# Token lists of a mixture-of-experts kernel built by one-hot matrix products instead of scatters, with the first expert's late columns in fp32 and a reordered start of the last layer

## The chip, the cores and the metric

One core of one Trainium2 chip. The metric is the device time of one execution in microseconds, as the median of several runs. Engines are named as in the profile: PE is TensorE (matmuls), DVE is VectorE, ACT is ScalarE, POOL is GpSimd, SP is SyncE, which here only issues DMAs.

## What is computed

Retention attention over 2 batches x 8 heads x 768 positions x 64, whose output, as 1536 tokens of 512 numbers, goes through a noisy top-2 mixture of eight experts (512 to 1024 to 512), and then through a dense layer with SoLU and layer norm. All in fp32.

```python
def _attn_ref(q, k, v):
    ...
    for t in range(S):
        state = gamma[None, :, None, None] * state + np.einsum('bhd,bhe->bhde', k[:, :, t], v[:, :, t])
        y[:, :, t] = scale * np.einsum('bhd,bhde->bhe', q[:, :, t], state)

def _moe_ref(x, w_gate, w_noise, noise, w1, w2):
    noisy_logits = x @ w_gate + np.log1p(np.exp(x @ w_noise)) * noise
    top2 = np.argpartition(-noisy_logits, 2, axis=1)[:, :2]
    ...
    for e in range(E):
        for k in range(2):
            mask = top2[:, k] == e
            h = np.maximum(x[mask] @ w1[e], 0.0)
            out[mask] += top2_w[mask, k, None] * (h @ w2[e])

def _moe2_ref(x, w_in, w_out, g_ln):
    h = x @ w_in
    e = np.exp(h - np.max(h, axis=-1, keepdims=True))
    solu = h * (e / (np.sum(e, axis=-1, keepdims=True) + 1e-09))
    ...
    ln = (solu - mu) / np.sqrt(var + 1e-06) * g_ln
    return ln @ w_out
```

## The kernel before

The 1536 tokens are twelve tiles of 128. The order of instructions on every engine is the order in which the program writes them; nothing is rescheduled. Each engine takes its own in order.

**Attention and routing.** A loop over the twelve tiles (i = 0 to 11) makes the scores, adds the running state, and lets `rows_logits` multiply by the gate (L461), store the rows of x to `xd` in DRAM and keep the logits. `choose` (L472 to L503) picks the top two of four groups of tiles: 0 to 3, 4 to 7, 8 and 9, 10 and 11. `rank` counts, with products against triangular and full matrices of ones, how many earlier tokens chose the same expert. `slots` (L589 to L603, seven VectorE operations) turns rank and expert into an address in a list `token_of` in DRAM, and `scatter` (L652) lets POOL write 128 token numbers of four bytes there, twice a tile, 24 times in all, each behind a one-element memset. `load_xg` (L959) later reads a list of an expert back (L968), scales it (L974), and gathers the tokens' rows of x by it (L983).

**The first expert** doesn't wait for its list. Its tokens of tiles 0 to 7 (192 columns, "early") and of tiles 8 to 11 (256, "late") are found by one-hot products: `first_rows` compares ranks with column numbers (L527, 16-bit one-hot tiles), `list_rows` (L530) multiplies them with token numbers (L539), POOL gathers (L548), TensorE transposes (L561). The early columns are multiplied in plain fp32 with the raw weights, four matmuls for each of eight steps f of the hidden layer (L671), while routing goes on. The late ones, like all other experts, use pairs of f32r numbers, hi and lo: twelve matmuls a step (hi x hi, hi x lo, lo x hi), with weights split by ScalarE (`wh`, L202) and VectorE (`wl`, L203). Each step's result leaves its PSUM bank as `hh` on ScalarE (L675) and `hl` on VectorE (L676); two banks `b` take turns. Then comes the second layer (`second`, L1038), between and behind whose parts the next expert's rows are transposed (L997).

**Seven more experts**, sorted by how many tokens they have, run the same way with a list each. The last one's second layer leaves rows (L1127, three blocks of 128 tokens, banks c3, c2, c0), stored by `y_rows` (L1110, L1112).

**Last layer.** POOL gathers each token's two expert rows (L766), `mix` weighs and adds them (ScalarE L776, VectorE L777), `x2_t` transposes (L786) and splits them (L789, L790), `h_in` multiplies by w_in (L805, 24 matmuls a tile in two halves), `solu_max`/`solu` (L810 to L824), `z_t` transposes (L858), `z_turn` (L869) does the same through DRAM for later tiles, `out_mm` multiplies by w_out (L915). The last four row blocks of w_out are scaled and split late, by `last_weights` (L901, L902), from two loads of 512 KB.

Weights come in units of 512 KB on SP's queue (`load_unit`, L184); `feed(split_to, load_to)` splits and loads up to given units.

## Time and profile before

| | us |
|---|---|
| median of 3 runs (lowest to highest) | 541.91 (539.79 to 543.49) |
| the profiled execution | 540.02 |
| its span, first to last instruction | 538.3 |
| TensorE busy in it | 504.6 (94%) |
| VectorE, ScalarE, POOL busy | 372.5, 218.7, 190.8 |
| mean granted TensorE clock | 0.974 |

All trace times below are from that one execution, counted from its first instruction; 1.7 us lie outside its span. [...]

### The profile page before, as it was taken

The numbers are of one execution on the slowest core, as the hardware profiler recorded it, in microseconds if no ns is written. First come the engines' busy times: TensorE is split into PE (matmuls) and PEld (weight loads), VectorE is DVE, ScalarE is ACT, GpSimd is POOL, SyncE is SP. The second block draws the span as 40 slices with busy tenths as digits, with TensorE's granted clock in tenths as the row PEclk, the third lists the DMA queues.
The fourth block names the chain that finished last, engine by engine and source line by source line (L and its number), as shares of the span: only waits on it lengthen the run. The fifth ranks groups of instructions, "written<-read, shape, count | busy, mean of one in ns | idle before, by whom it ended". The sixth has DMA issues, their size and how long they took to land.

```text
span 538.3 us, 8946 instructions
## 1 busy us (share of the span) xinstructions
PE 504.6 (94%) x3216; PEld 459.6 (85%) x3216; DVE 372.5 (69%) x742; ACT 218.7 (41%) x426; POOL 190.8 (35%) x287
## 2 busy tenths in 40 slices
PE   8998769399999999999999999999799999999995
PEld 7777659399999999999999999998577888888885
DVE  4468737277688968878988889886148865667640
ACT  4656215053432433424343434435235553343441
POOL 3015435657671732704827100000423523311120
PEclk9999959799999999999999999999989999999999
DMA  8996603468486674866876757666632665553331
GB/s 246 324 329 193 226 20 122 153 196 291 141 274 198 237 214 131 294 161 209 262 260 216 202 190 221 185 173 176 226 86 66 195 202 146 159 173 99 97 118 44
DMA packets 60130, 100.36 MB, mean 186 GB/s; under 512 B 10896, under 2 KB 28400, under 8 KB 60080
## 3 DMA queue, kind: packets, MB, share of 16 engines
q1 hardware_dynamic: 52720, 85.94, 50.7%
q0 software_dynamic: 6016, 13.44, 8.8%
q8 instruction: 27, 0.44, 0.3%
q10 hardware_dynamic: 1344, 0.34, 0.3%
q14 instruction: 23, 0.19, 0.1%
HBM read 76.99 MB, written 22.70 MB: 185 GB/s over the span
## 4 chain that ended last, share of the span: by engine, by line
PE 82%; DMA 6%; DVE 4%; another core or an unknown queue 3%; issue 2%; ACT 1%; POOL 0%; SPq 0%; POOLq 0%; ACTq 0%; DVEq 0%
PE c L1038 24%; PE b L671 14%; PE b L915 12%; PE a L671 12%; PE d L805 11%; PE c L461 2%; PE b L407 1%; DMA y<-yg,slot_y 1%; PE c L449 1%; PE c L1127 1%; DMA qt<-in_qT_dram 1%; PE a L786 1%; DMA xr<-xd,rows 1%; PE c L671 1%
## 5 line engine op out<-in xcount | busy, mean ns | idle before, releaser
L983 POOL DMA_INDIRECT xq<-xd,rows x78 | 91.2, 1169 | 65.9 <-issue 65.3
L203 DVE TENSOR_TENSOR wl<-wr,wh 128x1024 fp32r<-128x1024 f32 x68 | 81.5, 1218 | 3.7 <-ACT wh L202 3.2
L1038 PE MATMUL c<-hh,wh 128*128 128x448 f32 (+5 forms) x224 | 78.8, 352 | 0.0
L1038 PE MATMUL c<-hh,wl 128*128 128x448 f32 (+5 forms) x224 | 78.8, 352 | 0.0
L1038 PE MATMUL c<-hl,wh 128*128 128x448 f32 (+5 forms) x224 | 78.7, 352 | 0.0
L202 ACT ACTIVATE wh<-wr 128x1024 fp32r<-128x1024 f32 x68 | 69.9, 1050 | 6.5 <-DMA wr<-in_moe_w_dram 5.2
L766 POOL DMA_INDIRECT y<-yg,slot_y x24 | 23.6, 985 | 93.4 <-DMA yg<-y 87.8
L671 PE MATMUL b<-xh,wh 128*128 128x256 f32 (+7 forms) x144 | 48.4, 342 | 8.7 <-DVE hl L676 8.6
L671 PE MATMUL b<-xh,wl 128*128 128x256 f32 (+7 forms) x144 | 47.7, 337 | 0.0
L805 PE MATMUL d<-wh,x2h 128*128 128x512 f32 x96 | 40.0, 417 | 3.3 <-ACT x2h L789 3.3
L1038 PEld LDWEIGHTS c<-hh,wl 128*128 128x128 f32 x224 | 42.1, 188 | 1.1
L1038 PEld LDWEIGHTS c<-hh,wh 128*128 128x128 f32 x224 | 42.1, 188 | 1.1
L1038 PEld LDWEIGHTS c<-hl,wh 128*128 128x128 f32 x224 | 42.1, 188 | 1.1
L675 ACT ACTIVATE hh<-b 128x256 fp32r<-128x256 f32 (+8 forms) x40 | 18.5, 466 | 58.8 <-PE b L671 32.4
L805 PE MATMUL d<-wh,x2l 128*128 128x512 f32 x96 | 39.0, 406 | 0.0
L671 PE MATMUL a<-xh,wh 128*128 128x448 f32 (+6 forms) x112 | 38.9, 348 | 0.0
L805 PE MATMUL d<-wl,x2h 128*128 128x512 f32 x96 | 38.8, 405 | 0.0
L671 PE MATMUL a<-xh,wl 128*128 128x448 f32 (+6 forms) x112 | 38.8, 347 | 0.0
L1003 ACT ACTIVATE xh<-xt 128x428 fp32r<-128x428 f32 (+5 forms) x24 | 13.0, 540 | 58.7 <-DVE xt L1001 55.4
L676 DVE SCALAR_TENSOR_TENSOR hl<-b,hh 128x256 fp32r<-128x256 f32 (+8 forms) x40 | 20.9, 524 | 22.4 <-ACT hh L675 16.6
L671 PEld LDWEIGHTS b<-xh,wh 128*128 128x128 f32 x144 | 28.0, 194 | 9.5 <-DVE hl L676 9.1
L832 POOL TENSOR_SCALAR st<-st 128x1 f32<-128x1 f32 x12 | 2.5, 205 | 84.9 <-ACT ee L829 84.8
(226 smaller groups left out, 1110.6 us busy)
## 6 DMA issues: line engine op xcount, KB each, us to landing
wr<-in_moe_w_dram SPq DMA_DIRECT2D x64, 512.0 KB
zd<-zs SPq DMA_DIRECT2D x40, 128.0 KB
zc<-zd SPq DMA_DIRECT2D x10, 512.0 KB
raw<-in_moe_w_in_dram SPq DMA_DIRECT2D x8, 512.0 KB
raw<-in_moe_w_out_dram SPq DMA_DIRECT2D x8, 512.0 KB
yg<-yr SPq DMA_DIRECT2D x16, 208.0 KB
qt<-in_qT_dram SPq DMA_DIRECT2D x12, 256.0 KB
vt<-in_v_dram SPq DMA_DIRECT2D x12, 256.0 KB
```

Source lines behind the costliest of these rows:

```text
L202: nc.scalar.activation(hi, t, AF.Copy)
L203: nc.vector.tensor_sub(lo, t, hi)
L461: nc.tensor.matmul(rows[:, at:at + 128 + 2 * E], XT[i][:, s, k, :], unit[:, s, k, :], start=(k == 0), stop=(k == 1), skip_group_check=True)
L671: nc.tensor.matmul(p, w[:, 0, f * 128:(f + 1) * 128], x[:, d, c], start=(n == 0), stop=(n == len(terms) - 1))
L675: nc.scalar.activation(hh[:, f, c], p, AF.Relu)
L676: nc.vector.scalar_tensor_tensor(hl[:, f, c], p, 0.0, hh[:, f, c], op0=OP.max, op1=OP.subtract)
L766: nc.gpsimd.indirect_dma_start(out=t, out_offset=None, in_=yg[:upto], in_offset=bass.IndirectOffsetOnAxis(ap=slot_y[:, i, s:s + 1], axis=0))
L805: nc.tensor.matmul(PH[i][:, s, :], x[:, c], w[:, 0, f], start=(n == 0), stop=(n == 3 * KD - 1))
L915: nc.tensor.matmul(p, z[:, f * 128:(f + 1) * 128], w_rows(f, n)[:, c], start=(m == 0), stop=(m == len(terms) - 1))
L983: nc.gpsimd.indirect_dma_start(out=x[:, b] if e > 1 else xr_t[e][b], out_offset=None, in_=src[:], in_offset=bass.IndirectOffsetOnAxis(ap=r ...
L1003: nc.scalar.activation(hi, t, AF.Copy)
L1038: nc.tensor.matmul(py[d][:, :CAPS[e]], c, h[:, f, :CAPS[e]], start=(f == 0 and n == 0), stop=(f == KF - 1 and n == 2))
```

## The change

**Lists.** The scatters, `slots`, the DRAM list and its reads are gone. One PSUM bank ("books") holds ranks, counts and the first expert's row numbers, and in it 24 products of 128x128 one-hot tiles (L632) build all lists: for each tile and choice, `columns` makes two tiles of 16-bit numbers on VectorE, one with the token number where the list and set agree (L625), one with 1 where the place in the set agrees (L626). `places` prepares their scalars once for all tiles, `pick_rows` takes the second expert's rows (four operations) and then the others' (six) out of the bank. `turns` counts with one product instead of twelve. The columns are written between the first expert's late steps.

**First expert.** The late 256 columns are multiplied in fp32 with the raw weights too, so its four first-layer units are not split, and their raw tiles live in the buffers of `wl`. Its transposed rows are copied, not split. The second layer's four units are loaded during tiles 10 and 11. The second expert's transposes move from the fourth part of the second layer to behind parts 2, 3, 3 and 4.

**Last layer.** The third block uses bank c3 instead of c0. `mix(1)` stands behind the block loop, and so does the load of the last two weight units. The first half of `h_in(0)` takes the hi terms first. All `last_weights` come after `z_turn(1)`.

```diff
-        t = wraw.tile([128, a, n], F32, tag="wr", name="wr")
+        t = wsp.tile([128, a, n], F32, tag="wl", name="wr") if u < 4 else wraw.tile([128, a, n], F32, tag="wr", name="wr")
...
-    feed_at = [0, 0]
+    feed_at = [4, 0]
...
-        hi, lo = xgT[0]
         at = BLKS[2 * part][0]
-        nc.scalar.activation(hi[:, d:d + 2, at:at + 2 * n], p, AF.Copy)
-        nc.vector.tensor_sub(lo[:, d:d + 2, at:at + 2 * n], p, hi[:, d:d + 2, at:at + 2 * n])
-
-    xe = rt.tile([128, KD, EARLY], F32, name="xe", bufs=1)
-    ROWP, RK, x0, xgT = {}, {}, {}, {}
-
-    def rank(g, tag):
+        if d:
+            nc.scalar.activation(xe[:, d:d + 2, at:at + 2 * n], p, AF.Copy)
+        else:
+            nc.vector.tensor_copy(xe[:, d:d + 2, at:at + 2 * n], p)
+
+    xe = px.tile([128, KD, CAP], F32, tag="xh", name="xe")
+    x0, xgT = {}, {}
+    books = []
+    RK = None
...
+    def open_books():
+
+        nonlocal RK
+        p = bank("a1")
+        books.extend((p[:, 0:4], p[:, 4:100], p[:, 128:224], p[:, 256:384]))
+        RK = books[2].rearrange("p (i e) -> p i e", e=E)
...
-    def slots(g):
-        (t, pk), p = RT.pop(g), RK[g]
-        i0, m = GROUPS[g]
-        ii = slice(i0, i0 + m)
-        rk, at, spare = ranks[:, ii, :], t[:, 6, :m, :2], t[:, 7, :m, :2]
+
+    sq = const.tile([128, E, E], F32, name="sq")
+
+    def turns():
+
         V = nc.vector
-        V.tensor_mul(pk[:, :m], pk[:, :m], p[:, :, None, :].to_broadcast([128, m, 2, E]))
-        V.reduce_sum(rk, pk[:, :m], axis=AX.X)
-
-        V.tensor_scalar(sets[:, ii, :], rk, 1 / 32, -31 / 64, op0=OP.mult, op1=OP.add)
-        V.scalar_tensor_tensor(at, top_i[:, ii, :], ROOM / 16, rk, op0=OP.mult, op1=OP.add)
-        V.scalar_tensor_tensor(at, sets[:, ii, :], (1 - ROOM) / 16, at, op0=OP.mult, op1=OP.add)
-
-        V.scalar_tensor_tensor(spare, rk, float(ROOM), behind[:, ii, :], op0=OP.is_ge, op1=OP.mult)
-        V.scalar_tensor_tensor(slot[:, ii, :], at, 16.0, spare, op0=OP.mult, op1=OP.max)
...
+        nc.tensor.matmul(p, ones, chosen.rearrange("p i e -> p (i e)"), start=False, stop=True, skip_group_check=True)
...
+    def places():
+
+        V = nc.vector
+        full = [128, NT, 2, E]
+        pk = ep.tile([128, CAP], F32, tag="xt", name="pk", bufs=2)
+        pk = pk[:, :NT * 2 * E].rearrange("p (i s e) -> p i s e", s=2, e=E)
+        v = ep.tile([128, NT, 2], F32, name="v")
+        rj = ep.tile([128, NT, 2], F32, name="rj")
+        V.tensor_copy(top_i, ix[:, :, :2])
+        V.tensor_tensor(pk, e8[:, None, None, :].to_broadcast(full), top_i[:, :, :, None].to_broadcast(full),
+                        op=OP.is_equal)
+        V.tensor_mul(pk, pk, RK[:, :, None, :].to_broadcast(full))
+        V.reduce_sum(ranks, pk, axis=AX.X)
+        V.tensor_scalar(sets, ranks, 1 / 32, -31 / 64, op0=OP.mult, op1=OP.add)
+        V.scalar_tensor_tensor(rj, sets, -32.0, ranks, op0=OP.mult, op1=OP.add)
+        V.tensor_scalar(v, sets, 15.0, None, op0=OP.min)
+        V.scalar_tensor_tensor(v, top_i, 16.0, v, op0=OP.mult, op1=OP.add)
+        lw = ep.tile([128, 24, 128], F16, tag="yr", name="lw")
+        LS["v"], LS["rj"], LS["w"] = v, rj, lw
+
+    def columns(ks):
+        for k in ks:
+            i, s = divmod(k, 2)
+            o, w = LS["w"][:, k % 12], LS["w"][:, 12 + k % 12]
+            nc.vector.tensor_scalar(w, lane_h, LS["v"][:, i, s:s + 1], number_f[:, i:i + 1], op0=OP.is_equal, op1=OP.mult)
+            nc.vector.tensor_scalar(o, lane_4.rearrange("p a j -> p (a j)"), LS["rj"][:, i, s:s + 1], None, op0=OP.is_equal)
+            LS[k] = o, w
+
+    def lists(ks):
+        for k in ks:
+            i, s = divmod(k, 2)
+            nc.tensor.matmul(books[3], *LS.pop(k), start=False, stop=(k == 2 * NT - 1), skip_group_check=True)
+
+    def pick_rows(one):
+
+        V = nc.vector
+        got = books[3].rearrange("p (e b) -> p b e", b=16)
+        if one:
+            m, n = [128, 16, E], [128, 4, 4]
+            t = ep.tile([128, CAP], F32, tag="xt", name="t1", bufs=2)
+            t = t[:, :16 * E].rearrange("p (b e) -> p b e", e=E)
+            u = ep.tile([128, 16], F32, name="u1")
+            V.tensor_mul(t, got, sq[:, 1:2, :].to_broadcast(m))
+            V.reduce_sum(u, t, axis=AX.X)
+            u = u.rearrange("p (b c) -> p b c", c=4)
+            V.tensor_mul(u, u, own[:, None, :].to_broadcast(n))
+            V.reduce_max(rows1, u, axis=AX.X)
+            return
+        m = [128, 3, 16, E]
+        for n in (0, 3):
+            t = ep.tile([128, CAP], F32, tag="xt", name="t2", bufs=2)
+            t = t[:, :48 * E].rearrange("p (n b e) -> p n b e", b=16, e=E)
+            u = ep.tile([128, 3, 16], F32, tag="u2", name="u2")
+            V.tensor_mul(t, got[:, None].to_broadcast(m), sq[:, 2 + n:5 + n, None, :].to_broadcast(m))
+            V.reduce_sum(u, t, axis=AX.X)
+            V.tensor_scalar(rows2[:, n:n + 3], u, 4.0, part, op0=OP.mult, op1=OP.add)
...
-    def scatter(i):
-        for s in range(2):
-            nc.gpsimd.memset(spacer, 0.0)
-            st = nc.gpsimd.indirect_dma_start(
-                out=token_of[:], out_offset=bass.IndirectOffsetOnAxis(ap=slot[:, i, s:s + 1], axis=0),
-                in_=token[:, i:i + 1], in_offset=None)
-            for o in scat:
-                tc.declare_no_dep(st.ins, o.ins, reason="slots are distinct")
-            scat.append(st)
...
+        if e:
+            xh, xl = xgT[e]
+            terms = [(unit_t[8 * e + d][n], x, d) for x, ns in ((xh, (0, 1)), (xl, (0,))) for d in range(KD) for n in ns]
+        else:
+            terms = [(raw_t[d], xe, d) for d in range(KD)]
...
-    SCATTER = {6: (0,), 7: (1,), 8: (2,), 9: (3,), 10: (4,), 11: (5,)}
...
-        for n in SCATTER.get(i, ()):
-            scatter(n)
-        feed(0, max(0, min(2 * (i - 7), 4)))
+        feed(0, max(0, min(2 * (i - 7), 8)))
...
+        terms = [(x, d, n) for d in range(KD) for x, n in ((hi, 0), (hi, 1), (lo, 0))]
+        if s == 0 and i == 0:
+
+            terms.sort(key=lambda t: t[0] is lo)
...
     for f in range(KF):
         evacuate = hidden(0, f, slice(0, EARLY), ("c0", "c1", "b", "b")[f % 4])
         if f == 1:
-            list_rows(1, range(NT - 2), "a0")
+            list_rows(1, range(NT - 2))
         if f == 2:
-            rank(3, "c3")
+            rank(3)
             first_rows(3)
         if f == 3:
             list_rows(1, range(NT - 2, NT))
-            slots(2)
-            for n in range(7, 10):
-                scatter(n)
         evacuate()
-        if f > 2:
-            feed(min(f - 2, 4), 0)
-    feed(4, 8)
+        if f == 4:
+            route(2)
+            route(3)
+        if f == 5:
+            turns()
+        if f == 6:
+            places()
     for p in range(2):
         first_xt(1, 2 * p)
-    route(3)
-    slots(3)
-    scatter(10)
-    scatter(11)
-    turns()
...
+        if e == 1:
+            xr_t[e] = []
+            for b in range(4):
+                n = min(128, CAPS[1] - 128 * b)
+                t = px.tile([128, DM], F32, tag="xr", name="xr", bufs=4)
+                nc.gpsimd.indirect_dma_start(out=t[:n], out_offset=None, in_=xd[:],
+                                             in_offset=bass.IndirectOffsetOnAxis(ap=rows1[:n, b:b + 1], axis=0))
+                xr_t[e].append((t, n))
+            return
...
+        up = 8 * e + AHEAD[j] if e else 5 + j if j < 4 else 1 + 2 * j if j < 7 else 14
         if j > (3 if e else 1):
             convert()
-        feed(up, up + 3)
+        feed(up, up + (3 if e else 4))
...
+                if not e:
+                    columns(range(6 * f, min(6 * f + 6, 2 * NT)))
+                    lists(range(max(0, 6 * f - 6), min(6 * f, 2 * NT)))
+                    if f == 5:
+                        pick_rows(True)
+                        for _ in load_xg(1):
+                            pass
+                    if f == 6:
+                        pick_rows(False)
...
-            second(e, j, py, (0, 1) if j == 3 and not e else ())
-            for d in (((0, 1), (2,), (3,), ()) if e else ((), (), (), (2, 3)))[j]:
+            second(e, j, py)
+            for d in (((0, 1), (2,), (3,), ()) if e else ((), (0,), (1, 2), (3,)))[j]:
                 xg_t(e + 1, d)
...
-        py = bank(("c3", "c2", "c0")[b])
+        py = bank(("c3", "c2", "c3")[b])
...
-            feed(n_units - 2, n_units)
             mix(0)
-            mix(1)
+    mix(1)
+    feed(n_units - 2, n_units)
...
     solu(0)
-    last_weights((0, 1))
     x2_t(2)
     h_in(1, 0)
     h_in(1, 1)
@@ -1153,7 +1160,7 @@
     z_t(0)
     solu(1)
     z_turn(1)
-    last_weights((2, 3))
+    last_weights(range(4))
```

Of the order of instructions, POOL between the last scatters and the gathers of the third expert (before): `xr` and `xq` are gathered rows of x, `token_of` is the list in DRAM.

```order
L654 MEMSET spacer 1x1
L655 DMA token_of<-token,slot 7168x1
L968 DMA rows<-token_of,at_r 128x4
L983 DMA xr<-xd,rows 128x512 x4
L968 DMA rows<-token_of,at_r 128x16
L974 TENSOR_SCALAR rows<-rows,part 128x16
L983 DMA xq<-xd,rows 128x128 x14
```

The same place after the change, from the last operation of attention on:

```order
L390 TENSOR_TENSOR vs<-vt,dec 128x256 x11
L535 DMA xr<-xd,rows_166 96x512 x2
L535 DMA xr<-xd,rows_166 128x512 x2
L980 DMA xr<-xd,rows_248 128x512 x3
L980 DMA xr<-xd,rows_248 64x512
L989 DMA xq<-xd,rows_249 128x128 x78
```

The spacers, scatters, list reads and scalings are gone; what remains are the gathers.

VectorE, before, from the end of `turns` over the first expert's late steps (`hl` is a step's low half, `wl` a weight's):

```order
L619 TENSOR_TENSOR keys<-best,over 128x8
L620 TENSOR_REDUCE short<-keys 128x1
L621 TENSOR_REDUCE spill<-short 128x1
L676 SCALAR_TENSOR_TENSOR hl<-b,hh 128x256 x4
L203 TENSOR_TENSOR wl<-wr,wh 128x1024
L676 SCALAR_TENSOR_TENSOR hl<-b,hh 128x256 x2
L203 TENSOR_TENSOR wl<-wr,wh 128x1024
L676 SCALAR_TENSOR_TENSOR hl<-b,hh 128x256 x2
```

And after, at the end of the columns (`lw` are the one-hot tiles, `a_787` the bank of lists, `rows_248` the second expert's rows):

```order
L625 TENSOR_SCALAR lw<-lane_h,v,number_f 128x128
L626 TENSOR_SCALAR lw<-lane_173,rj 128x128
L200 TENSOR_TENSOR wl<-wr,wh 128x1024
L703 SCALAR_TENSOR_TENSOR hl<-b,hh 128x256 x2
L643 TENSOR_TENSOR t_1555<-a_787,sq 128x128
L644 TENSOR_REDUCE u_1556<-t_1555 128x16
L646 TENSOR_TENSOR u_1556<-u_1556,own 128x16
L647 TENSOR_REDUCE rows_248<-u_1556 128x4
L200 TENSOR_TENSOR wl<-wr,wh 128x1024
L703 SCALAR_TENSOR_TENSOR hl<-b,hh 128x256
```

The late steps' `hl` now stand among 48 `lw` operations and the taking out of the rows, and fewer `wl` stand there.

ScalarE, before, at the end of the last expert (`y<-c` empties a block's bank, `t` is the mix of tile 0, then tile 1, `x2h` the transposed rows of tile 0, then tile 1):

```order
L1110 ACTIVATE y<-c_4320 128x4x4x32
L776 ACTIVATE t<-y_4308,top_w 128x512
L776 ACTIVATE t<-y_4312,top_w 128x512
L789 ACTIVATE x2h<-a_4380 128x512
L1110 ACTIVATE y<-c_4358 128x4x4x32
L789 ACTIVATE x2h<-a 128x512
```

And after:

```order
L1118 ACTIVATE y<-c_4210 128x4x4x32
L796 ACTIVATE t<-y_4198,top_w 128x512
L809 ACTIVATE x2h<-a_4263 128x512
L1118 ACTIVATE y<-c_4241 128x4x4x32
L796 ACTIVATE t<-y_4202,top_w 128x512
L809 ACTIVATE x2h<-a 128x512
```

The second `t` moved from ahead of the first `x2h` to behind it and behind the third block's `y`.

## Rows read from the trace of the kernel before

**Rows 1.** The page, part 4: the chain, share of the span by engine.
```profile
PE 82%; DMA 6%; DVE 4%; another core or an unknown queue 3%; issue 2%; ACT 1%; POOL 0%; SPq 0%; POOLq 0%; ACTq 0%; DVEq 0%
```

**Rows 2.** Busy time of each engine in five stretches (start:end us).
```profile
core 0: us, PE busy (x) PEld busy (x) DVE busy (x) ACT busy (x) POOL busy (x), PEclk, DMA share, GB/s
40.00:50.00 10.00, 8.57 (x145) 7.30 (x144) 9.36 (x38) 5.77 (x24) 5.68 (x10) 1.00 0.75 240
70.00:80.00 10.00, 6.73 (x24) 6.04 (x25) 4.13 (x24) 2.04 (x8) 2.13 (x5) 0.50 0.08 27
90.00:100.00 10.00, 4.89 (x46) 4.26 (x44) 6.55 (x29) 1.72 (x4) 8.26 (x16) 1.00 0.89 324
120.00:370.00 250.00, 250.00 (x1344) 244.69 (x1343) 206.00 (x339) 97.64 (x143) 98.51 (x87) 1.00 0.69 214
390.00:400.00 10.00, 10.00 (x39) 7.96 (x39) 2.74 (x4) 2.01 (x3) 3.96 (x4) 0.78 0.43 125
```

**Rows 3.** Chain of waits, 55 to 140 us (start, length, what).
```profile
67.94 6.23 another core or an unknown queue
...
92.75 10.45 another core or an unknown queue
...
114.95 17.02 PE c L1038 x84
```

**Rows 4.** Timeline of POOL, 58 to 105 us (start, length, instruction).
```profile
62.68 1.03 POOL L655 DMA_INDIRECT token_of<-token,slot  x1 [0.18 <-issue]
...
71.61 0.96 POOL L655 DMA_INDIRECT token_of<-token,slot  x1 [0.22 <-issue]
...
88.78 1.13 POOL L655 DMA_INDIRECT token_of<-token,slot  x1 [0.23 <-issue]
...
100.55 0.96 POOL L655 DMA_INDIRECT token_of<-token,slot  x1 [0.22 <-issue]
```

**Rows 5.** Timeline of DVE, 55 to 90 us.
```profile
57.14 1.07 DVE L527 TENSOR_SCALAR oh<-col_h,s 128x448 f16<-128x448 f16 x4
58.13 0.18 DVE L481 TENSOR_TENSOR lg<-lgs 128x32 f32<-128x32 f32 x1
...
63.73 0.21 DVE L595 TENSOR_TENSOR pk<-pk,a 128x64 f32<-128x64 f32 x1
...
64.87 0.17 DVE L485 SCALAR_TENSOR_TENSOR rt<-rt 128x16 f32<-128x16 f32 x1
...
83.73 0.48 DVE L527 TENSOR_SCALAR oh<-col_h,s 128x256 f16<-128x256 f16 x2
84.12 0.35 DVE L676 SCALAR_TENSOR_TENSOR hl<-b,hh 128x192 fp32r<-128x192 f32 x1
```

**Rows 6.** Timeline of PE, 76 to 93 us.
```profile
76.83 4.50 PE L671 MATMUL c<-xe,wr 128*128 128x192 f32 x16
...
87.53 2.76 PE L671 MATMUL b<-xe,wr 128*128 128x192 f32 x16
...
92.31 0.39 PE L671 MATMUL b<-xh,wh 128*128 128x256 f32 x1
```

**Rows 7.** The page, part 5: the group of weight splits on DVE.
```profile
L203 DVE TENSOR_TENSOR wl<-wr,wh 128x1024 fp32r<-128x1024 f32 x68 | 81.5, 1218 | 3.7 <-ACT wh L202 3.2
```

**Rows 8.** Timeline of PE, 385 to 405 us.
```profile
388.46 0.80 PE L805 MATMUL d<-wh,x2h 128*128 128x512 f32 x1 [3.29 <-ACT x2h L789]
...
394.14 0.72 PE L786 MATMUL a<-ident,t 128*128 128x128 f32 x4
...
397.49 0.60 PE L786 MATMUL a<-ident,t 128*128 128x128 f32 x4
...
404.95 0.66 PE L858 MATMUL a<-ident,z 128*128 128x128 f32 x4 [0.84 <-DVE x2l L790]
```

**Rows 9.** Chain of waits, 370 to 425 us.
```profile
379.76 7.36 DMA y<-yg,slot_y
```

**Rows 10.** Timeline of DVE at 403 us.
```profile
402.89 1.41 DVE L902 SCALAR_TENSOR_TENSOR xl<-wr,gcol,xh 128x512 fp32r<-128x512 f32 x2
```

More of the change, by code (lines that the diff above doesn't have):

```diff
@@ L493, in choose @@
         V.tensor_add(nl, nl, lg[:, :, :E])
-        ix = rt.tile([128, 4, 8], U32, tag="ix", name="ix", bufs=3)
         for n in range(m):
@@ L538, in list_rows @@
                 at, n = BLKS[2 * part + b]
-                nc.tensor.matmul(p[:n, b:b + 1], OH[i][:, at:at + n], number[:, i:i + 1], start=(i == 0 and b == 0),
+                nc.tensor.matmul(p[:n, b:b + 1], OH[i][:, at:at + n], number[:, i:i + 1], start=False,
                                  stop=last, skip_group_check=True)
@@ L557, in first_xt @@
         n = BLKS[2 * part][1]
-        p = bank("ab"[1 - part], (128, 2, 2 * n)) if n <= 128 else None
+        p = bank(f"c{2 + d // 2}" if part else "b", (128, 2, 2 * n))
         for s in range(2):
@@ L623, in weights @@
+    rows1 = const.tile([128, 4], U32, name="rows1")
+    rows2 = const.tile([128, E - 2, 16], U32, name="rows2")
     def weights():
@@ L927, in retnet_moe_solu @@
     hidden_of(0)
-    route(3)
-    route(2)
-    route(3)
-    route(3)
-    scatter(6)
-    raw0 = [raw_t[d] for d in range(KD)]
+    for n in range(3):
+        route(3)
     for f in range(KF):
@@ L994, in xg_t @@
             t = bank("a")
[L995 to L997 removed]
+            for b, (x, n) in enumerate(xr_t[e]):
+                nc.tensor.transpose(t[:, 128 * b:128 * b + n], x[:n, d * 128:(d + 1) * 128], ident[:n, :n])
         else:
@@ L1027, in y_t, with second @@
             PY.pop(e)
-    def second(e, j, py, between=()):
+    def second(e, j, py):
         hh, hl = H_t[e]
```

169 lines of the change are left out of this document (58 added, 111 removed).

## Prediction

> **What bounds the kernel now.** I read the page's chain by engine first, then the windows of engine time, then the chain of waits piece by piece where TensorE is idle, and last the timelines of single engines. The chain says that TensorE sets the end for 82% of the span, and that 3% stands against "another core or an unknown queue" [rows 1]. There is only one core, so those 3% are waits whose releaser the profile could not name, and they deserve a look. The windows show where TensorE is not busy: from 120 to 370 us it is busy 250.00 of 250.00 us at granted clock 1.00, but only 6.73 of 10 in 70 to 80, at 0.50, and 4.89 of 10 in 90 to 100; 390 to 400 is full but at 0.78 [rows 2]. The middle, seven experts, therefore gives nothing unless TensorE gets less to do there, and the change leaves its matmuls alone. What can be won lies in three places: the end of attention, the first expert's late columns, and the step from the last expert to the last layer.
>
> The chain of waits gives the two unnamed pieces: 6.23 us from 67.94 and 10.45 us from 92.75, together 16.7 us [rows 3]. In both, VectorE and ScalarE wait for TensorE results whose matmuls had been issued before. Both lie inside a burst of scatters on POOL: the first burst starts at 62.68 with eight scatters and its last one at 71.61, the second at 88.78 with ten and its last at 100.55 [rows 4]. The first unnamed piece ends at 74.17, the second at 103.20, each some 2 us after its last scatter began. That is a coincidence in time seen twice, not a mechanism; no row says why a list write on POOL should hold TensorE's results. It is not the DMA engines' time: in 70 to 80 their share is 0.08 [rows 2]. It is not POOL's indirect DMAs as such: POOL is busy 98.51 us in the experts, with gathers, and TensorE has no gap there [rows 2].
>
> [...]
>
> **The change part by part.** The sums are made against the profiled execution, 540.02 us.
>
> *End of attention.* All 24 scatters go. The 6.23 us piece should go with them. The seven VectorE operations that made scatter addresses go too: at tile 11 they take VectorE from 63.73 to 64.87, 1.14 us [rows 5], in front of the routing chain that ends just where the unnamed piece begins, so they are on the path. The same seven stand at tile 6, where VectorE is busy 9.36 of 10 us [rows 2]; I count 0.8 of those 1.1. In their place an index search of four tiles moves from tile 10 to tile 11, on the same crowded engine, which I count as even. Together 8.2 us. From below: if only the stall goes and the search costs what the slots did, 6.2; from above, both sets of slots in full, 8.5. The two weight units of the second layer that are now loaded during tiles 10 and 11 are on SP's queue among the x stores; that queue carries only what is needed later, so I count nothing; if a store that a gather needs came 1 us later it would cost that 1 us.
>
> *First expert, early columns.* Same matmuls. Sixteen of them take 4.50 us at 76.83, right after the idle stretch, and 2.76 us at 87.53 [rows 6]; the first falls in the window with granted clock 0.50 [rows 2], the lower of the two levels. With 6 us less idle time ahead, this slow group may run at the upper level, up to 1.7 us; I take 0.7, since some 3 us of waiting on the routing chain stay. After the last of them, the late columns start at 92.31 [rows 6] once the gathered rows have come; the rows' cast stands at the same place between the same matmuls, so this distance is kept.
>
> *First expert, late columns.* Before, they run from 92.31 to 114.95, where the second layer starts [rows 3, 6]: 22.64 us with the 10.45 us piece in it, so about 12.2 of work, 0.127 for each of 96 matmuls. Now each of the eight steps is four fp32 matmuls of 256 columns in place of twelve in two halves. From the early columns (2.76/2 = 1.38 us for 192) I estimate 1.38 x 256/192 = 1.84 us a step, 14.7 for eight, 2.5 more than before. Twenty-four list products of 128 columns come in between; at half of 0.127 that is 1.5, so TensorE has 16.2 us of work. The splits of the four first-layer units go, VectorE and ScalarE each have four large operations less; VectorE gets 48 column operations instead. Their price no row shows. The nearest rows are the one-hot operations of the old kernel on 16-bit tiles: four of 448 columns take 57.14 to 58.13, 0.25 each from start to start, two of 256 take 83.73 to 84.12, 0.195 each [rows 5]. On a straight line 128 columns give 0.16; bounds are 0.12, if the fixed part is less, and 0.24, the whole 0.48 of the pair halved. I take 0.16: 48 x 0.16 = 7.7 us. Beside them VectorE has to put out eight hl tiles (0.35 for 192 columns [rows 5], about 0.42 for 256, so 3.4), a copy, and two weight splits of 1.22 [rows 7] before the last steps' banks come free. That is 13 to 14 us, less than TensorE's 16.2, but each step's columns feed the next step's products, and two banks only let TensorE run two steps ahead; I add 2.2 us for handing over. 18.4 against 22.64: 4.2 us gained. With 0.24 for a column it is 3.8 worse and the gain nearly gone (0.4); without any handing over it is 6.4.
>
> [...]
>
> *Second expert's rows.* Its gathers now wait for four small operations after the last column, not for the list read and the scatters. By the steps above the first is issued some 16 us after the late columns start (six steps of eight, and those four operations). POOL issues such transfers 1.28 us apart [rows 4], so the fourth goes at 20, and lands 4 to 7.4 us later (the upper end is the slow gather of [rows 9]), at 24 to 27.4. The first transpose that needs them stands behind 48 matmuls of the second layer, at 17.02/84 each 9.7 us [rows 3], so 28.1 after that start. Covered; if the columns cost 0.24 the second layer moves with them and the cover stays.
>
> *The end of the experts.* The first layer of the last FFN waits 3.29 us at 388.46 for ScalarE's x2h [rows 8]. On ScalarE the second tile's mix stands ahead of x2h in order, and that mix waits for a gather which took 7.36 us, until 387.12 [rows 9]. Now x2h(0) is ahead, its transposes stand in front of the last block's last three matmuls, and the 3.29 go. The hi terms come first, so x2l is not waited for either. The twelve matmuls then run from 388.46 to 394.14, 5.68 us, in a window of clock 0.78, while the next twelve with four transposes need 3.35, to 397.49 [rows 2, 8]. With no idle stretch ahead they should stay at the upper level: about 2.8 instead of 5.68, 2.9 won. The pair of late weight operations, 1.41 us on VectorE at 402.89 [rows 10], stood ahead of the x2l for which TensorE waits 0.84 at 404.95 [rows 8]; moved behind z_turn(1) it lets the 0.84 go. What is late next: all four late weights now follow each other there, 4 x 0.71, while the output layer begins; it reads them from its ninth matmul on, and by my count the last comes 0.4 too late. Their loads are issued later than before, behind the last block's store on SP, and have the first two tiles' matmuls to land in. The mix(1) gather, without 1 MB of loads beside it, should come sooner, but if it still landed at 387.1, x2_t(1) would stay covered by the first half tile. 3.3 + 2.9 + 0.8 - 0.4 = 6.6 us; from 4, if the clock falls all the same, to 7.5.
>
> **Sum.** 8.2 + 0.7 + 4.2 + 6.6 = 19.7. On the profiled execution 540.02 - 19.7 = 520.3. The median of the runs, 541.91, is 1.9 above it, so 522.2 on that scale. Its own range, from the bounds above, is 517 to 527.
>
> **Rivals.** *The stalls stay.* If something else holds TensorE's results (the x stores, weight loads, instruction supply), the 6.23 comes back, and about 8 in the late columns, where the rest lies beside the longer work: 522.2 + 14 = 536.5 or so. If one of the two stays, about 530. For it: no row names the releaser. Against it: two bursts, two stalls, each ending with its burst, and none elsewhere. 0.12, half for each.
>
> *The lists become the bound.* VectorE's columns at 0.24, and TensorE waits on each step: 522.2 + 3.8 = 526.0, some 528 if the second expert's rows also come late. For it: the columns are more than half of VectorE's work there. Against it: the starts of the one-hot operations [rows 5]. 0.12.
>
> *Slower: the column operations cost what operations with a per-partition scalar cost elsewhere.* Both kinds of column read one or two such scalars. The old kernel's L902, with one, takes 1.41 for two, 0.71 each [rows 10], though on 512 columns of fp32. At 0.71 the 48 take 34 us on VectorE in place of 7.7: 26.4 more, all in front of the second layer, and 548.6. It decides from 19.7/48 + 0.16 = 0.57 us a column on. Against it: L527 reads such a scalar too and starts every 0.195. 0.04.
>
> **How the numbers follow.** 0.72 for the forecast, 0.12, 0.12 and 0.04 for the rivals. A measurement of this kernel tells about 1%, 5.4 us, from no change, so faster means below 536.5. Forecast, list rival and half of the first rival are faster, 0.90; the other half counts as the same, 0.06; the rest, 0.04, is slower. The range from 516 to 530 holds the forecast, the list rival and part of the one-stall case.
>
> **What would show it.** Right: no unnamed piece above 1 us before 130 us; the early matmuls starting near 68; the second layer near 102; no wait ahead of the last FFN's first matmul, and clock 1.00 behind it. Wrong: a piece of 5 us or more there with POOL idle; columns more than 0.25 us apart; TensorE idle in front of the second expert's transposes; a window below 0.9 after the last block.

## The result, and the profile after

The chip compared the two kernels at 0.9715 of the time before (95% interval 0.966 to 0.9771): faster. The profiled execution took 520.34 us, its span is 518.5 and its mean granted clock 0.994; the sum had ended at 520.3 for it. That is not the whole result. Of the twelve runs of the changed kernel five lie from 520.34 to 526.84 and seven from 534.38 to 551.67, so that their median is 537.19, beside 539.03 (535.05 to 543.49, twelve runs) before; the comparison leaves the seven out as disturbed, and what happens in such a run is taken up with the experiments, because it turned out to be made by this kernel and curable.

The chain by engine, on the page of the changed kernel, answers to [rows 1]: no unnamed queue is left in it.

```profile
PE 93%; DVE 4%; DMA 1%; issue 1%; ACT 0%; POOL 0%; DVEq 0%; ACTq 0%
```

The windows of engine time answer to [rows 2], with one more stretch (start:end us; busy us of each engine, then granted clock, DMA share, GB/s):

```profile
core 0: us, PE busy (x) PEld busy (x) DVE busy (x) ACT busy (x) POOL busy (x), PEclk, DMA share, GB/s
70.00:80.00 10.00, 8.09 (x54) 7.43 (x53) 6.99 (x36) 2.25 (x6) 1.92 (x2) 1.00 0.20 62
90.00:100.00 10.00, 9.19 (x47) 7.48 (x47) 8.81 (x31) 3.54 (x8) 1.22 (x1) 1.00 0.50 157
120.00:370.00 250.00, 250.00 (x1327) 242.85 (x1326) 202.23 (x333) 98.37 (x144) 83.00 (x74) 1.00 0.68 207
370.00:380.00 10.00, 8.57 (x44) 6.72 (x43) 3.63 (x5) 3.02 (x5) 4.03 (x5) 1.00 0.80 258
390.00:400.00 10.00, 10.00 (x50) 8.18 (x49) 8.54 (x14) 5.55 (x11) 5.01 (x9) 1.00 0.50 153
```

The reader is to see TensorE's granted clock at 1.00 in both stretches where it was 0.50 and 0.78; in 70 to 80 it is busy 8.09 us instead of 6.73, in 90 to 100 9.19 instead of 4.89. The experts stay full.

The timeline of TensorE from the last tiles of attention to the late columns (start, length, instruction, in brackets the wait ahead of it) answers to [rows 6]:

```profile
50.06 1.16 PE L404 MATMUL b<-qt,kt 64*128 64x128 f32 x16
51.15 0.19 PE L573 MATMUL a<-chosen,before 128*128 128x32 bf16 x1
...
54.98 1.16 PE L404 MATMUL b<-qt,kt 64*128 64x128 f32 x16
...
60.79 1.40 PE L548 MATMUL b<-ident,xr 96*128 96x96 f32 x8 [1.43 <-DMA xr<-xd,rows]
...
64.66 2.96 PE L698 MATMUL c<-xe,wr 128*128 128x192 f32 x16
...
79.69 2.64 PE L698 MATMUL b<-xe,wr 128*128 128x256 f32 x11 [1.76 <-DVE xe L554]
```

L404 are the scores of one tile: in the changed kernel these two tiles follow each other by 4.92 us, and the rank product (L573) stands behind the scores without a wait. The early columns start at 64.66, before at 76.83, and sixteen matmuls take 2.96 there instead of 4.50. Two waits are new: 1.43 for the gathered rows (`xr`), and 1.76 for the copy `xe` in front of the late columns.

The timeline of VectorE there answers to [rows 5]; of the columns (`lw`) the first three of 48 are shown, 0.22 and 0.16 us apart:

```profile
76.70 0.17 DVE L609 CAST top_i<-ix 128x24 f32<-128x24 uint32 x1
...
78.96 0.68 DVE L554 COPY xe<-c 128x512 f32<-128x512 f32 x1
...
82.48 0.31 DVE L625 TENSOR_SCALAR lw<-lane_h,v,number_f 128x128 f16<-128x128 f16 x1
82.70 0.25 DVE L626 TENSOR_SCALAR lw<-lane,rj 128x128 f16<-128x128 f16 x1
82.86 0.31 DVE L625 TENSOR_SCALAR lw<-lane_h,v,number_f 128x128 f16<-128x128 f16 x1
```

A pair of columns takes 0.38 us from start to start, 0.19 each. Ahead of the copy `xe` at 78.96 stand the operations of `places`, from 76.70 on: they are most of what the 1.76 waits for, beside the copy itself (0.68).

The chain of waits, from the first late step to the second expert, answers to [rows 3] (start, length, what):

```profile
79.69 2.01 PE b L698 x8
...
84.11 0.22 DVE lw L625
...
94.24 5.24 PE b L698 x24
99.48 9.73 PE c L1043 x48
...
121.68 2.63 PE b L698 x12
```

From 81.73 to 94.24 the chain runs mostly through VectorE, with column after column in it: in all 8.6 of the 19.8 us of the late columns are `lw`. The second layer starts at 99.48, before at 114.95; the second expert at 121.68, before at 136.15 by the same view, with no wait in front. At the end of the experts, the chain and the one row of TensorE's timeline with a wait answer to [rows 8, 9]:

```profile
372.18 0.61 ACT y L1118
...
372.83 3.07 PE d L825 x12
...
392.09 5.50 PE b L935 x24
```

```profile
372.83 0.50 PE L825 MATMUL d<-wh,x2h 128*128 128x512 f32 x1 [1.43 <-ACT y L1118]
```

TensorE meets the last layer at 372.83 after a wait of 1.43 for `y`, the copy that empties bank c3 of the third block. The output layer starts at 392.09 with no wait, 19.26 us later; before, it was 411.64 - 388.46 = 23.18 (the first start is in [rows 8], the second is the old timeline's).

### The profile page after: what moved, and what is told of

Read it like the earlier page. It is cut to its first block, busy times and chain, and to the rows that moved or that the text cites. A ratio compares the mean times of both kernels' runs of the same rounds, so it can differ in the third digit from the quotient of the medians.

```text
span 518.5 us, 8865 instructions
## 1 busy us (share of the span) xinstructions
PE 504.2 (97%) x3197; PEld 456.4 (88%) x3197; DVE 375.4 (72%) x769; ACT 214.4 (41%) x421; POOL 153.6 (30%) x225
## 4 chain that ended last, share of the span: by engine, by line
PE 93%; DVE 4%; DMA 1%; issue 1%; ACT 0%; POOL 0%; DVEq 0%; ACTq 0%
PE c L1043 25%; PE b L698 14%; PE d L825 13%; PE b L935 13%; PE a L698 12%; PE c L1135 3%; PE c L458 3%; PE b L404 2%; PE c L446 2%; PE c L698 1%; PE a L806 1%; DMA xr<-xd,rows 1%; PE a L432 1%; DVE lw L625 1%; PE c L421 1%; PE c L262 1%
## 5 line engine op out<-in xcount | busy, mean ns | idle before, releaser
L200 DVE TENSOR_TENSOR wl<-wr,wh 128x1024 fp32r<-128x1024 f32 x64 | 76.7, 1218 | 1.1 <-ACT wh L199 0.8
L199 ACT ACTIVATE wh<-wr 128x1024 fp32r<-128x1024 f32 x64 | 65.4, 1049 | 0.0
L702 ACT ACTIVATE hh<-b 128x256 fp32r<-128x256 f32 (+8 forms) x40 | 18.7, 468 | 52.2 <-PE b L698 45.2
L698 PE MATMUL b<-xh,wh 128*128 128x448 f32 (+6 forms) x112 | 39.1, 349 | 0.0
L698 PE MATMUL a<-xh,wh 128*128 128x448 f32 (+6 forms) x112 | 39.0, 348 | 0.0
L698 PE MATMUL b<-xh,wl 128*128 128x448 f32 (+6 forms) x112 | 38.8, 347 | 0.0
L698 PE MATMUL a<-xh,wl 128*128 128x448 f32 (+6 forms) x112 | 38.8, 347 | 0.0
L825 PE MATMUL d<-wh,x2l 128*128 128x512 f32 x96 | 37.4, 395 | 0.0
L702 ACT ACTIVATE hh<-a 128x448 fp32r<-128x448 f32 (+6 forms) x28 | 14.4, 513 | 46.6 <-PE a L698 33.7
L838 ACT ACTIVATE ee<-d,st 128x1024 f32<-128x1024 f32 x12 | 13.4, 1116 | 40.3 <-DVE st L831 37.2
```

Of the source, the lines that this page charges most:

```text
L199: nc.scalar.activation(hi, t, AF.Copy)
L200: nc.vector.tensor_sub(lo, t, hi)
L698: nc.tensor.matmul(p, w[:, 0, f * 128:(f + 1) * 128], x[:, d, c], start=(n == 0), stop=(n == len(terms) - 1))
L702: nc.scalar.activation(hh[:, f, c], p, AF.Relu)
L825: nc.tensor.matmul(PH[i][:, s, :], x[:, d * 128:(d + 1) * 128], unit_t[8 * E + d][n][:, 0, f], start=(m == 0), stop=(m == len(terms) - 1))
```

## The experiments

Theory after the result: the scatters held TensorE's results, and without them the holds are gone; the lists cost a little more than forecast. Rivals: something else in the burst's neighbourhood held them (POOL's work, the rows' stores), or only the size of the writes matters. "After" below means the changed kernel.

**The scatters put back into the changed kernel**, at their old places, to a list that nobody reads (24 scatters, and copies in place of the address arithmetic):

```diff
+        for n in SCATTER.get(i, ()):
+            scatter(n)
...
+    scatter(6)
...
+            slots(2)
+            for n in range(7, 10):
+                scatter(n)
...
+    scatter(10)
+    scatter(11)
...
```

> The changed kernel with the 24 scatters put back at their old places (behind their memsets, to a DRAM list that nothing reads, addresses by four small VectorE copies where the slots stood). If the scatters hold TensorE's results, both unnamed waits come back, in attention's end and in the late columns, some 6 and 8 us, and the time rises by 12 to 16 us, near 533 to 537 on the profiled execution. If the scatters only coincided with the waits, the time stays within 2 us of the changed kernel's 520.

Measured: 545.18 in the profiled execution, four runs from 545.18 to 572.65, 1.0141 of before (1.0069 to 1.0213). Chain of waits:

```profile
95.02 2.12 another core or an unknown queue
...
99.98 3.58 issue
```

The unnamed piece and the 3.58 "issue" are the holds again, now in the late columns. The last scatter on POOL began at 102.54 and took 0.96, to 103.50; TensorE goes on at 103.56. The hold at the end of attention did not come back as one piece: TensorE stops there many times between its matmuls, by 0.2 to 2.3 us each, and the gather of the early rows lands in 10.12 us, where the changed kernel has 5.16. The early columns started at 77.94, the second layer at 123.66, 24 us behind the changed kernel, where 12 to 16 had been expected. So the scatters are the cause, and cost more in the new order than in the old.

**The scatters alone taken out of the kernel before:**

```diff
-        for n in SCATTER.get(i, ()):
-            scatter(n)
```

(and the three other calls; the lists in DRAM stay zero, so that the later experts all gather token 0)

> The kernel before with all 24 scatters left out; the lists in DRAM stay zero, so the later experts gather token 0. If the scatters hold TensorE's results, both unnamed waits vanish and 12 to 16 us go, to 524 to 528 on the profiled execution. If something else holds them, the waits stay and the time stays within 2 us of 540.

Measured: 525.02 (523.71 to 528.2, four runs), 0.9751 (0.9699 to 0.9803). Its chain:

```profile
68.66 4.05 PE c L671 x16
...
98.05 17.02 PE c L1031 x84
...
119.25 2.43 PE b L671 x12
```

No unnamed piece is left. The second expert starts at 119.25, 16.9 us ahead of before (136.15); the two holds of [rows 3] had 16.7. The two don't match place by place: the early columns start 8.4 us sooner, where the piece had 6.23. This is also the measure of the new first expert, its lists and its fp32 late columns together: early columns to second layer take 29.4 us here (68.66 to 98.05) and 34.8 in the changed kernel (64.66 to 99.48), which starts its early columns earlier and yet meets the second expert 2.4 us later. Without the scatters the old order would have had the whole gain at the front and more; lists and late columns give some 5 us of it back.

**The third block back in bank c0:**

```diff
-        py = bank(("c3", "c2", "c3")[b])
+        py = bank(("c3", "c2", "c0")[b])
```

> The changed kernel with the last expert's third block in bank c0 as before. If TensorE's 1.43 us wait for ScalarE's y ahead of the last layer is for bank c3, which the last layer's first half reuses, it goes and the time falls by 1.4 us. If it is for x2h or the pool, it stays.

Measured: 524.53 (522.3 to 543.95, four runs), 0.972 (0.9664 to 0.9775). In the chain the last layer now follows the block directly, with neither the `y` copy nor a wait between:

```profile
377.21 0.70 PE c L1135 x3
377.91 3.05 PE d L825 x12
```

The wait came from the bank. The total doesn't show the 1.4 us, because this execution is later elsewhere: its second layer starts at 103.15, 3.7 us behind, after a gather of the early rows that took 6.04 us (5.16 in the changed kernel) and early matmuls that took 3.93 us for the first sixteen (2.96); and one wait of 1.4 us without a releaser stands in the experts.

**Columns, list products and the taking out left out**, with rows of zero, so that every expert but the first gathers token 0:

```diff
-                    columns(range(6 * f, min(6 * f + 6, 2 * NT)))
-                    lists(range(max(0, 6 * f - 6), min(6 * f, 2 * NT)))
...
-                        pick_rows(True)
...
-                        pick_rows(False)
```

> The changed kernel without columns, list products and the taking out of rows (48, 24 and 10 instructions); all later experts gather token 0. If the lists bound the late columns, the stretch from the first late matmul to the second layer falls from 19.6 us to TensorE's own, 8 x 1.84 to 8 x 1.9 = 15, and the time by 4 to 5 us. If hl and the weight splits bound it, less than 1 us.

Measured: 533.99 (528.06 to 535.21, four runs), slower than the changed kernel's 520.34 with less work. The chain tells why:

```profile
80.00 8.50 PE b L700 x32
...
89.85 3.62 another core or an unknown queue
...
93.88 2.48 another core or an unknown queue
...
97.71 5.77 another core or an unknown queue
...
103.88 7.36 another core or an unknown queue
...
116.60 15.12 DMA wr<-in_moe_w_dram
```

The first late steps go undisturbed. Since the rows are ready at once, POOL issues the gathers of three experts from 74.57 on, 1.25 us apart but for a few pauses, and then four unnamed pieces hold TensorE, 19.2 us together. Behind them 15.12 us go by on a weight load. As a price of the lists this run failed; but it shows the hold without one scatter, with gathers of rows. It is not a clean case of it: from 100 to 112 the DMA engines are busy 0.96 of the time at only 97 GB/s (changed kernel 0.80 at 273), so that the run of gathers and slow transfers stand side by side here. It first cast doubt on the prediction's sentence that POOL's indirect DMAs as such are harmless; the unedited kernel below decides it.

**The kind of transfer.** Two kernels put, in place of the scatters, gathers of four-byte numbers from a table, and scatters of 128 rows of 512 bytes; a third put three small multiplications on POOL for each scatter, with no DMA:

```diff
+            nc.gpsimd.indirect_dma_start(
+                out=got_t[:, i, s:s + 1], out_offset=None, in_=token_of[:],
+                in_offset=bass.IndirectOffsetOnAxis(ap=slot[:, i, s:s + 1], axis=0))
...
```

> The changed kernel with 24 gathers of 128 four-byte numbers from DRAM into SBUF where the scatters stood, same memsets, same addresses, nothing reads them. If it is POOL's indirect DMAs with tiny elements as such that hold TensorE's results, the waits come back as with the scatters put back (543 on the profiled execution, 24 us above the changed kernel). If only writes into DRAM do it, the time stays within 4 us of 520 to 525.

```diff
+                out=token_of[:], out_offset=bass.IndirectOffsetOnAxis(ap=slot[:, i, s:s + 1], axis=0),
+                in_=ident[:], in_offset=None)
...
```

> The changed kernel with 24 scatters of 128 rows of 512 bytes each (one constant tile into an unread DRAM array) where the four-byte scatters stood. If it is the four-byte size that holds TensorE's results, the waits don't come back and the time stays within 4 us of 520 to 525; if scatters of any size do it, it rises to some 540 or more.

```diff
+            for _ in range(3):
+                nc.gpsimd.tensor_tensor(busy, busy, busy, op=OP.mult)
...
```

> The changed kernel with three small POOL multiplications in place of each of the 24 scatters, so POOL is as busy but issues no DMA there. If POOL's DMAs hold TensorE's results, no unnamed waits come in attention's end or the late columns, and the time stays within 4 us of the changed kernel. If a busy POOL does it, some 540 as with the scatters.

Measured: the tiny gathers 530.48 and 543.86, the wide scatters 531.31 and 548.61, too few runs for a verdict. One trace of each shows holds at the old places, smaller than with the scatters put back: unnamed pieces of 3.53 us with the tiny gathers and of 2.61 with the wide scatters ahead of the late columns, whose second layers start at 110.34 and 108.28, between the changed kernel's 99.48 and 123.66. So neither writing nor the four bytes are needed for a hold; how much the size matters is not settled. The profiled execution of the tiny gathers, the one of 543.86, has its largest holds elsewhere, at the second expert, where it has the changed kernel's own gathers:

```profile
130.47 12.48 another core or an unknown queue
...
144.46 9.76 another core or an unknown queue
```

The multiplications took 533.88 (525.69 to 542.91, four runs); no hold stands at the scatters' places, and the second layer starts at 100.67, 1.2 us behind the changed kernel, so busy POOL without DMA does nothing there. But this kernel too has one at the second expert:

```profile
120.05 4.87 another core or an unknown queue
```

That stretch is word for word the changed kernel's: POOL gathers for three experts in one run. This hold ends at 124.92, in the middle of the run; from 134 to 144 TensorE then stops eight more times between its matmuls, 6.4 us together.

**The changed kernel once more**, without an edit, to look at a long execution:

> The changed kernel once more, beside the others on one chip. If its late gather of the first expert's early rows or another transfer varies from execution to execution, its profile differs from the first one (518.5 span) in the wait for those rows or in the late columns; if not, span and waits agree within 1 us.

Measured: six runs from 521.15 to 547.09; the profiled one took 547.09. One stretch holds most of the difference to 521.15. TensorE's timeline there (L1002 is a transpose, L698 the second expert's first layer):

```profile
125.45 0.69 PE L1002 MATMUL a<-ident,xr 128*128 128x128 f32 x4
...
127.19 0.37 PE L698 MATMUL b<-xh,wl 128*128 128x448 f32 x1
145.46 0.74 PE L698 MATMUL b<-xh,wh 128*128 128x448 f32 x1 [17.90 <-issue]
```

On ScalarE the copy that reads this transpose comes 18.7 us after its end (125.45 + 0.69):

```profile
144.86 0.54 ACT L1008 ACTIVATE xh<-a 128x448 fp32r<-128x448 f32 x1 [20.12 <-remote]
```

POOL meanwhile issues gathers, 21 of them in this stretch, 1.25 us apart for the most part; the first and the last stand here:

```profile
117.36 1.43 POOL L989 DMA_INDIRECT xq<-xd,rows  x1 [0.30 <-issue]
...
143.29 0.94 POOL L989 DMA_INDIRECT xq<-xd,rows  x1 [0.30 <-issue]
```

And the windows, with the columns as above:

```profile
120.00:128.00 8.00, 7.56 (x38) 6.24 (x36) 4.79 (x6) 2.99 (x4) 6.17 (x7) 1.00 0.75 253
128.00:144.00 16.00, 0.00 (x0) 0.00 (x0) 0.00 (x0) 0.00 (x0) 12.04 (x14) 0.57 0.36 113
```

From 128 to 144 TensorE, VectorE and ScalarE stand still, POOL alone works, with the DMA engines at 0.36, and the others go on 0.6 us after the last gather, which ends at 144.23. The copy starts at 144.86, after 20.12 us of waiting for a releaser that the view gives as "remote": whether TensorE's word comes late or the product itself is not shown, for the ends of matmuls are modelled. It doesn't look like instruction supply, which the prediction had named among what might hold TensorE: no packet of an instruction queue moves from 128 to 144. In the kernel before, from 68 to 74, all 160 packets are of POOL's queue: neither a store of x nor a weight load nor an instruction moves in the first hold. It is [rows 3] and [rows 4] again at another place. In the kernel before, list reads broke the gathers here into groups (one read at 112.55, the next gather at 118.70); the changed kernel issues 4 + 14 + 13 of them without a pause, from 103.03 to 143.29. In the changed kernel's profiled execution of 520.34 the same 31 stand between 98.57 and 144.26, and TensorE waits for nothing there; they are 1.52 us apart on average there, several of them taking 1.9 to 2.0 us on POOL, where in the hold all are 1.25 apart. Which of the two makes the other the traces don't tell.

**The gathers paced.** If the run is the cause, a pause every two gathers that follows the experts' progress must take the long executions away:

```diff
+                if e < 4:
+                    nc.gpsimd.tensor_copy(pace, unit_t[max(unit_t)][1][:1, 0, :1])
...
```

(one element of the newest weight split is copied ahead of each pair of gathers for the third and fourth expert)

> The changed kernel with the gathers for the third and fourth experts paced: before each pair, POOL copies one element of the newest split weight, so a pair goes out with each step of the experts instead of 31 gathers one behind the other. If a run of POOL's indirect DMAs is what holds TensorE's results (18 us in one execution, until the run's last gather), the slow executions of 532 to 552 vanish, all lie within 520 to 528 and the median falls by some 10 us. If the hold comes from elsewhere, the spread stays.

Measured: 521.67, five runs from 521.26 to 522.59, 0.9713 (0.9692 to 0.9734). POOL's timeline, and the windows of the stretch above:

```profile
106.49 0.18 POOL L992 COPY pace<-wl 1x1 f32<-1x1 f32 x1 [3.32 <-DVE wl L200]
106.83 0.98 POOL L993 DMA_INDIRECT xq<-xd,rows  x1 [0.16 <-issue]
...
114.40 0.18 POOL L992 COPY pace<-wl 1x1 f32<-1x1 f32 x1 [5.34 <-DVE wl L200]
```

```profile
120.00:128.00 8.00, 8.00 (x42) 7.19 (x41) 5.99 (x11) 3.68 (x6) 6.64 (x9) 1.00 0.73 240
128.00:144.00 16.00, 16.00 (x81) 14.83 (x80) 13.10 (x21) 6.51 (x10) 13.60 (x16) 1.00 0.74 217
```

POOL waits 3.32 and 5.34 us for VectorE's splits; the later copies up to 144 find theirs done and only stand between the pairs. TensorE is busy 16.00 of 16 us where it had 0.00. Of 18 runs of the changed kernel 10 were above 532; of the 11 paced ones, this kernel and the last below, none is above 523. The kernel with multiplications, unpaced and on the same chip, spread to 542.91, so it isn't the chip.

**Two repairs at the lists and the bank**: `places` behind the copy `xe`, 16 of the 24 L626 on POOL, the third block in c0; first unpaced, then with the pauses:

```diff
-            nc.vector.tensor_scalar(o, lane_4.rearrange("p a j -> p (a j)"), LS["rj"][:, i, s:s + 1], None, op0=OP.is_equal)
+            (nc.gpsimd if k % 6 in (1, 2, 4, 5) else nc.vector).tensor_scalar(o, lane_4.rearrange("p a j -> p (a j)"), LS["rj"][:, i, s:s + 1], None, op0=OP.is_equal)
...
```

> The changed kernel with bank c0 for the third block, the scalars of the columns made behind the copy of the late rows instead of ahead of it, and 16 of the 24 one-scalar columns on POOL, which is idle there. If VectorE's columns bound the late steps, the late columns start 1 us sooner and take some 17 us instead of 19.6, and with the bank's 1.4 us the time falls by 4 to 5 us below the changed kernel's. If POOL's columns are slow (0.5 us each or more), TensorE waits for them and nothing is gained but the bank's 1.4.

> The paced gathers together with bank c0, the later scalars and 16 columns on POOL. If pacing removes the holds and the other three their 1.4, 1 and 2 us, all executions lie near 515 to 520; if not, they spread from 516 to 540 as before.

Measured: unpaced 516.74 to 540.01 (four runs, median 533.95, a 7.5 us wait at the second expert in the profiled one); paced 518.25 (515.76 to 521.45, six runs), 0.965 (0.962 to 0.9681), the best version tried. The wait for `xe` fell from 1.8 to 0.3 us. A column costs 0.73 us on POOL on average (sixteen in 11.68), and TensorE waited 1.3 us for those.

**The scatters of the kernel before spaced out**, three multiplications instead of a memset between them:

```diff
-            nc.gpsimd.memset(spacer, 0.0)
+            for _ in range(3):
+                nc.gpsimd.tensor_tensor(spacer, spacer, spacer, op=OP.mult)
...
```

> The kernel before with three small POOL multiplications instead of one memset between scatters, so that they go out half as often. If scatters hold TensorE's results only where they follow each other closely, the 6.2 and 10.5 us waits shrink and the time falls below 536 unless the later lists cost it again; if each scatter does its share, the waits stay or grow with the burst, to 545 or more.

Measured: 549.73 (548.54 to 559.76, five runs), 1.0246 (1.0215 to 1.0278). The trace is of the longest, 559.76. TensorE's waits from 40 to 150 us (engine, line, waited for, total, times, longest):

```profile
PE a L999 <- DMA xr<-xd,rows: 5.9, 3, 5.6
PE a L582 <- DVE chosen L497: 5.8, 2, 3.8
PE a L561 <- DMA xr<-xd,rows: 4.1, 2, 3.7
```

With the scatters 2.2 us and more apart, no wait of 6 or 10 us is left at their places; the longest there are 3.8 for the routing chain and 3.7 for the late rows. But the last scatter begins at 110.86 instead of 100.55, the list is read later, and the second expert's rows come too late (L999, 5.6 us). It agrees with the run as the cause, and shows that spacing alone is no cure where the list itself is waited for.

## Why the prediction was right, and where it was wrong

The total was right for the five shorter executions alone: the forecast of 522.2, with 517 to 527, was for the median of the runs, and those five, from 520.34 to 526.84, have 524.58; the median of all twelve, 537.19, lies outside the range. The main mechanism was right: the two unnamed pieces belonged to the bursts of scatters and went with them (both experiments with scatters agree), and the rival that the stalls stay fell for these places. Term by term, in one execution each:

- *End of attention*, forecast 8.2: the early columns start 12.2 us earlier (76.83 to 64.66). Two things were missed. The scatters cost more than the named piece: in the kernel before without them the early columns start at 68.45, so 8.4 of the 12.2 are theirs, not 6.2. I had read two bursts; an earlier one of six scatters, from 43.67 on, cost 1.0 (the tile that starts at 60.07 starts at 59.03 without them). The other 3.8 are the slots, forecast 2.0, and a move in the diff that I overlooked: the rank product now stands behind the next tile's scores.

```diff
-        if i == 9:
-            rank(1, "a1")
...
+        scores(i + 1)
...
+        if i == 9:
+            rank(1)
```

  Before, it stood ahead of them and waited for VectorE, twice, here for the second time (kernel before):

```profile
53.27 0.18 PE L582 MATMUL a<-chosen,before 128*128 128x32 bf16 x1 [0.94 <-DVE chosen L497]
```

- *Early columns*, forecast 0.7: 0.5. The clock gave more (sixteen matmuls 2.96 instead of 4.50, at a granted clock of 0.93 from 64.66 to 67.60 where it had been 0.61 from 76.83 to 81.30; in windows of half a microsecond the kernel before has 0.50 from 67.0 to 80.0 and 1.00 from 80.5 to 100), but `places` stands in front of `xe` on VectorE, and TensorE waits 1.76 for it. I priced those operations nowhere.
- *Late columns*, forecast 22.64 to 18.4: 99.48 - 79.69 = 19.8. The term mis-sized is the column: 0.19 us each, where I took 0.16, the straight line, inside my bounds of 0.12 and 0.24; 24 pairs at 0.38 make 9.1 us. I had also let TensorE's 16.2 us end last, with 2.2 for handing over; the chain runs through VectorE's columns for most of the stretch instead. In mechanism that is the rival "the lists become the bound", at a lower price than its 0.24.
- *Second expert*: the rows came in time, as forecast, but the second layer takes 22.2 us instead of 21.2, counted as nothing: its sixteen transposes now stand in three groups instead of two, and take 0.5 longer in the chain, the matmuls around them another 0.5.
- *The end of the experts*, forecast 6.6: 5.3. The 3.29 wait became 1.43, not nothing, because the third block and the last layer's first bank meet in c3; I read ScalarE's order and not the banks. The first half tile is 3.07 instead of 5.68, 2.6 won where 2.9 had been forecast. The late weights made TensorE wait nowhere. The seven experts took 0.7 longer.

The sum, 12.2 + 0.5 + 2.8 - 1.0 + 5.3 = 19.8, is the difference of the spans, 538.3 - 518.5. The forecast of 19.7 was so near by luck: 4 us at the end of attention that I hadn't counted covered four terms that I put too high. The upper end of the range doesn't follow from the bounds either: the lowest gains, 6.2, 0, 0.4 and 4, would leave 531 and not 527.

One step failed outright: "It is not POOL's indirect DMAs as such: POOL is busy 98.51 us in the experts, with gathers, and TensorE has no gap there." In the old kernel those gathers were broken up by list reads. Without them the hold came back at the second expert: 17.9 us of it in the one long execution of the changed kernel that has a trace, 22.2, 7.5 and 4.9 in the long ones of three other unpaced kernels (tiny gathers, columns on POOL, multiplications), and with the pauses no long execution was left in eleven. That the other nine long runs are of this kind follows from that, not from traces of their own. The sentence beside it, that it is not the DMA engines' time, looked at the first stretch alone; in 90 to 100 their share was 0.89 [rows 2]. There the experiments decided, and not that row. The rival "the stalls stay" was right about a hold, at a place where I hadn't looked for one.

Open: by what path a run of indirect DMAs on POOL holds what other engines see of TensorE's results, why only in some executions, why some holds end with the run and others in the middle of it, and how much the size of a row matters.

## What to carry to other kernels

A piece of waiting that no queue owns up to, beside a run of indirect DMAs on POOL, is a reason to suspect that run, even where the same run does no harm in another execution (here 520.34 and 547.09 us): take it out once to see (here 525.02 instead of 539.02), or break it up, for instance by letting POOL wait for the progress of whoever consumes the rows, and judge the cure by the spread of several runs (here 521.26 to 522.59 instead of 520.34 to 551.67), not by one. When a change removes something that also served as a pause, ask what now follows back to back (here 31 gathers). And when work moves from DMA to many small VectorE operations, take their price from start to start, at their own size, not from a straight line through larger ones (here 0.19 us, and 0.16 from the line), and count every one that stands ahead of the next evacuation (here a wait of 1.76 us).

## What had not been expected of the hardware

Beside a run of indirect DMAs on POOL, 1.25 to 1.27 us apart, ScalarE and VectorE can be kept from going on with matmuls that TensorE had been issued long before: 17.9 us, ending with the last of 31 gathers, while the DMA engines were busy 0.36 of the time. With the scatters put back TensorE itself was held in the middle of its matmuls, 3.58 us, to 0.06 after the last scatter. The same run in another execution of the same kernel held nothing: 520.34 and 547.09 us. POOL needs 0.73 us on average (sixteen in 11.68) for a column operation on 128 x 128 16-bit numbers; VectorE starts its columns every 0.16 to 0.22.
